# Choosing score banks for VectorE by a build-time account, queueing their later passes, and pairing row tiles in every filler step

## The chip, the cores and the metric

The kernel runs on one core of one Trainium2 chip. The metric is the time of one execution on the device, in microseconds, as the median of several runs; all seven inputs come from HBM and the output goes back there. A profile is one execution recorded by the hardware profiler. It has a span (first to last instruction) and a time of its own, which is a little longer than the span.

The engines are TensorE (PE in the profile, with its weight loads as PEld), VectorE (DVE), ScalarE (ACT), GpSimd (POOL) and SyncE (SP), which here only issues transfers. Each works through its own queue in order; they meet at semaphores that the framework sets from the tiles that instructions read and write.

## The reference

A transformer block on 2048 rows of 512 columns: layer norm, attention with 32 heads of 16, a residual, layer norm, a gated feed-forward part of 1792, a residual.

```python
qkv = (ln(x) @ wqkv)                       # 2048 x 1536 -> q, k, v, 32 heads of 16
p   = softmax(q k^T * 16 ** -0.5)          # 32 x 2048 x 2048
h   = x + (p v) @ wo
g, u = ln(h) @ w_gate, ln(h) @ w_up        # 2048 x 1792 each
out = h + (sigmoid(g) * u) @ w_down
```

The 32 x 2048 x 2048 exponentials, 134 million of them, are most of the elementwise work.

## The kernel before

**Steps.** Scores are made transposed, 128 keys by 512 queries at a time; such a piece fills one bank of PSUM. A unit is one head with one piece of keys (for the last two chunks of 256 queries, two pieces of keys, still one bank). Three units make a group, and the loop at the end of the program takes one group per step: 683 steps. `emit_scores` (from L746) writes one step: the score matmuls into one of two PSUM tiles `pss` of three banks, and one `activation` with Exp on ScalarE (L776) that turns the banks into bf16 probabilities in one of seven slots (`pt`, and pieces of `wd`, `stg` and `QTu` that lie idle at the time, so one line shows under several names). ScalarE works on one `pss` while TensorE fills the other.

**Cycles.** Four steps make a cycle. The twelve units of a cycle meet their values in three `emit_pv` calls (L839), which `plan_pv` puts six steps after the cycle's first: twelve matmuls, four at a time side by side in the array (tile position by columns), which add into the PSUM tile `acc`. A P.V matmul waits for the probabilities it reads. When a group of four heads is done, `emit_norm` (L816) copies `acc` out with VectorE (L820), and transfers bring the row sums through HBM and back.

**Filler.** Everything else that needs TensorE is a generator, `filler`, which yields a cost before each matmul: V tiles, K and Q projections, and for each chunk of queries the output projection, gate, up and down products. `emit_fill` draws from it at the end of each step, by a rate per step of the cycle (L737; 2, 2, 0 and 3 matmuls, none in the step of P.V) and by pauses ("gap", "at") that the generator asks for. All filler results go through one PSUM buffer, `pm`, which VectorE or ScalarE must empty before the next is started. The order of work on each queue is the order in which the program writes it; nothing reorders it later.

**Pairs.** A head has 16 columns, and a row of `QB` and `KT` for the bound, so the operands of two heads fit into the two halves of the 128 rows. Where `pairs` is set (L751), a score matmul takes 64 rows of the array at a tile position, and two of them from different halves run at once; otherwise it takes all 128 rows, with zeros for the other heads. Before, pairs are used in the first 44 steps, in every odd step, and in the third step of cycles that are in `twice`, except in the first two steps of a cycle with no filler (`idle`).

**Banks on VectorE.** ScalarE is relieved of some banks. In a step in `split` the activation takes two banks and VectorE makes the third's exponential by its own arithmetic, in five passes: the scores are scaled so that adding a constant and converting to an integer gives the bits of a power of two (`exp_bits`, L795), then the mantissa is cut out (L798) and a cubic is applied to it (L801, L804, L808). The first pass reads PSUM, so TensorE can't fill that `pss` again until it is done. `split` has the first step of each cycle, and `twice` adds the third step in every third or fourth cycle of some stretches. The later passes are put at fixed steps: one, two and three steps after the first, with `later`.

```python
split = set(range(8, G1, CYC))
...
later(i + 1, lambda: exp_first(*scratch))
later(i + 2, lambda: exp_second(*scratch))
later(i + 3, lambda: exp_third(pt[:, na, :], *scratch))
```

The intermediate results of the five passes lie in scratch space: one set for the first step of a cycle, and one in the `OT` tile not in use for the third.

## Time and profile before

| | |
|---|---|
| median of the runs | 966.58 us (966.09 to 969.06) |
| the profiled execution | 967.7 us, span 965.9 us |
| ScalarE busy | 897.1 us, 93% of the span |
| TensorE busy | 837.0 us, 87% |
| VectorE busy | 788.7 us, 82% |
| mean granted TensorE clock | 0.996 |
| banks on VectorE | 191 of 2048 |

A group's line in the profile gives the line of the kernel, the engine and operation, what it writes and reads with its shape and how often; then the busy time and the mean of one in ns; then the engine's idle time before these instructions, and what ended it. A busy engine can be one that waits inside a queue for nothing; what counts is which engine's idle time is short where the time is spent. TensorE's busy time counts each matmul with its whole latency, so matmuls that overlap in the array are merged, and a busy share of 90% is not the array at its peak. A window's line gives the same busy times for a stretch of time; the 40-step stretches of this kernel last 49 to 60 us.

A timeline's line gives the start, the time from the first's start to the last's end of a run of equal instructions, and in brackets how long the engine was idle before and what released it.

### The profile page before, as it was taken

To read this page: it belongs to the slowest core of one execution; us is meant where nothing else is said; L and a number is where in the kernel's file an instruction comes from. 1 tells how busy PE (TensorE), PEld (TensorE's weight loads), DVE (VectorE), ACT (ScalarE), POOL (GpSimd) and SP (SyncE) were. 2 spreads that over 40 slices of the span, in tenths; PEclk is the share of its full clock that TensorE was granted. 3 is DMA by queue.
4 is the path that set the end of the run, shared out by engine and by line. 5 is a ranking of instruction groups with operands and counts; after the bars stand their busy time and mean duration, and the time that the engine had idled before them with its cause. 6 is when DMAs were issued, how large, how long until landed. Compare 5 with 4: busy or idle time off the path is not lost.

```text
span 965.9 us, 17209 instructions
## 1 busy us (share of the span) xinstructions
PE 837.0 (87%) x6409; PEld 334.2 (35%) x6409; DVE 788.7 (82%) x1423; ACT 897.1 (93%) x770; POOL 39.0 (4%) x45
## 2 busy tenths in 40 slices
PE   4888888888889899988789999988788999998988
PEld 2221222222223232222222233222255555456646
DVE  8389999888888888898888888888898788777653
ACT  4799999999999999999999999989998999899862
POOL 4600000000000000000000000000000000000000
PEclk9999999999999999999999999999999999999999
DMA  5002341000003000001000000000010000110010
GB/s 161 20 1 56 114 95 38 15 15 3 15 26 103 15 15 16 16 12 27 15 26 27 16 16 16 12 17 26 16 29 24 16 12 13 27 32 16 9 35 12
DMA packets 37357, 28.39 MB, mean 29 GB/s; under 512 B 17692, under 2 KB 32632, under 8 KB 37272
## 3 DMA queue, kind: packets, MB, share of 16 engines
q1 hardware_dynamic: 35684, 25.71, 10.1%
q10 hardware_dynamic: 1588, 1.58, 0.5%
q8 instruction: 50, 0.82, 0.4%
q14 instruction: 35, 0.29, 0.1%
HBM read 20.31 MB, written 2.61 MB: 24 GB/s over the span
## 4 chain that ended last, share of the span: by engine, by line
PE 41%; DVE 26%; ACT 24%; issue 6%; DMA 2%; SPq 0%; ACTq 0%; DVEq 0%; POOL 0%
PE pss L765 20%; ACT pt L776 13%; PE acc L846 8%; PE pm L514 6%; ACT stg L776 4%; ACT wd L776 4%; DVE stg L795 3%; PE pm L530 3%; ACT QTu L776 2%; PE pm L490 2%; DVE st L137 2%; DVE reg L798 2%; DVE pt L808 2%; DVE y L801 2%; DVE y L804 2%
## 5 line engine op out<-in xcount | busy, mean ns | idle before, releaser
L765 PE MATMUL pss<-QB,KT 64*128 64x512 bf16 (+3 forms) x2560 | 473.2, 338 | 85.7 <-ACT pt L776 40.1
L776 ACT ACTIVATE pt<-pss 128x1536 bf16<-128x1536 f32 (+1 forms) x392 | 500.4, 1360 | 18.1 <-PE pss L765 14.8
L765 PEld LDWEIGHTS <-KT 64*128 64x128 bf16 (+1 forms) x2560 | 179.0, 95 | 345.4 <-issue 235.2
L776 ACT ACTIVATE stg<-pss 128x1536 bf16<-128x1536 f32 (+1 forms) x140 | 183.1, 1356 | 5.0 <-PE pss L765 4.2
L795 DVE TENSOR_SCALAR stg<-pss 128x512 int32<-128x512 f32 x123 | 84.8, 689 | 72.4 <-PE pss L765 60.5
L846 PE MATMUL acc<-pt,Vaug 128*17 128x512 bf16 (+1 forms) x1471 | 112.8, 339 | 5.8 <-DVE xs_all L820 3.7
L776 ACT ACTIVATE wd<-pss 128x1536 bf16<-128x1536 f32 (+1 forms) x80 | 103.8, 1392 | 1.4 <-PE pss L765 1.3
L776 ACT ACTIVATE QTu<-pss 128x1024 bf16<-128x1024 f32 (+1 forms) x71 | 95.5, 1345 | 1.7 <-PE pss L765 1.2
L801 DVE SCALAR_TENSOR_TENSOR y<-reg 128x512 f32<-128x512 f32 x123 | 85.2, 692 | 4.2
L804 DVE SCALAR_TENSOR_TENSOR y<-y,reg 128x512 f32<-128x512 f32 x123 | 84.2, 685 | 1.1
L846 PEld LDWEIGHTS <-Vaug 128*17 128x17 bf16 x2560 | 50.4, 89 | 97.4 <-issue 82.6
L530 PE MATMUL pm<-wd,reg 128*128 128x512 bf16 x224 | 62.4, 385 | 2.3 <-DVE ob L535 1.8
L514 PE MATMUL pm<-reg,reg 128*128 128x512 bf16 (+1 forms) x280 | 58.0, 337 | 6.4 <-DVE reg L527 6.2
L514 PE MATMUL pm<-reg,wu 128*128 128x512 bf16 (+1 forms) x280 | 58.1, 338 | 1.5 <-ACT sg L519 1.2
L798 DVE TENSOR_SCALAR reg<-stg 128x512 int32<-128x512 int32 x123 | 52.0, 423 | 2.0
L144 POOL TENSOR_TENSOR rs<-ve,pw_neg 128x1 f32<-128x1 f32 (+1 forms) x24 | 16.5, 687 | 894.5 <-DVE ve L142 893.9
L846 PE MATMUL acc<-stg,Vaug 128*17 128x256 bf16 (+1 forms) x564 | 50.7, 326 | 0.8 <-DVE stg L808 0.4
L527 DVE SCALAR_TENSOR_TENSOR reg<-sg,pm 128x512 bf16<-128x512 f32 x56 | 38.2, 683 | 14.5 <-PE pm L514 13.8
L808 DVE SCALAR_TENSOR_TENSOR pt<-y,stg 128x512 bf16<-128x512 f32 x70 | 47.8, 683 | 1.8
L519 ACT ACTIVATE sg<-pm 128x512 f32<-128x512 f32 x56 | 35.5, 633 | 10.3 <-PE pm L514 10.0
L795 DVE TENSOR_SCALAR wd<-pss 128x512 int32<-128x512 f32 x45 | 30.9, 687 | 13.0 <-PE pss L765 12.7
L163 PE MATMUL pm<-reg 128*128 128x512 bf16 x124 | 37.1, 387 | 1.2 <-DVE km L171 0.7
(115 smaller groups left out, 707.0 us busy)
## 6 DMA issues: line engine op xcount, KB each, us to landing
rb_all<-rd SPq DMA_DIRECT2D x96, 64.0 KB
reg<-in_A_x_dram SPq DMA_DIRECT2D x8, 256.0 KB
xr<-in_A_x_dram SPq DMA_DIRECT2D x16, 128.0 KB
out_dram<-ob SPq DMA_DIRECT2D x16, 128.0 KB
rb_all<-rd SPq DMA_DIRECT2D x60, 32.0 KB
KT<-stg SPq DMA_DIRECT2D x7, 256.0 KB
reg<-in_B_w_gate_dram SPq DMA_DIRECT2D x4, 448.0 KB
wu<-in_B_w_up_dram SPq DMA_DIRECT2D x4, 448.0 KB
```

The costliest lines, as they stand in the source:

```text
L163: nc.tensor.matmul(ps[:], lhsT=wqkv_sb[:, c, w0:w0 + P], rhs=xnT[:, c, n * QC:(n + 1) * QC], start=(c == 0), stop=(c == DC - 1))
L514: nc.tensor.matmul(ps[:, i * w:(i + 1) * w], lhsT=wt[:, c, f * P:(f + 1) * P], rhs=hnT[:, c, 0:w], start=(c == 0), stop=(c == DC - 1))
L527: nc.vector.scalar_tensor_tensor(out=out, in0=a, scalar=1.0, in1=b, op0=ALU.add, op1=ALU.mult)
L530: nc.tensor.matmul(ps[:], lhsT=hT[:, f, tt * P:(tt + 1) * P], rhs=wd[:, f, :], start=(f == 0), stop=(f == FC - 1))
L765: nc.tensor.matmul(pss[:, ui, h * w:(h + 1) * w], lhsT=KT[rows, g, kt * P:(kt + 1) * P], rhs=QB[n_qg % 2][rows, j, 0:w], start=True, stop= ...
L776: ex = nc.scalar.activation(out=pt[:, 0:na, :], in_=pss[:, 0:na, :], func=ACT.Exp, scale=DH ** -0.5 / QS)
L795: return nc.vector.tensor_scalar(out=e_bits, in0=src, scalar1=ONE_BITS, scalar2=0.0, op0=ALU.add, op1=ALU.max)
L798: nc.vector.tensor_scalar(out=e_man, in0=e_bits, scalar1=0x7FFFFF, scalar2=-0x40800000, op0=ALU.bitwise_and, op1=ALU.bitwise_or)
L801: nc.vector.scalar_tensor_tensor(out=e_pol, in0=m, scalar=PA, in1=m, op0=ALU.add, op1=ALU.mult)
L804: nc.vector.scalar_tensor_tensor(out=e_pol, in0=e_pol, scalar=PB, in1=e_man.bitcast(FP32), op0=ALU.add, op1=ALU.mult)
L808: nc.vector.scalar_tensor_tensor(out=dst, in0=e_pol, scalar=PC, in1=e_bits.bitcast(FP32), op0=ALU.add, op1=ALU.mult)
L846: nc.tensor.matmul(acc[32 * j:32 * j + VW, 0:w], lhsT=Vaug[:, kt, 4 * g + j, :], rhs=p[:, h * w:(h + 1) * w], start=(kt == 0), stop=(kt == ...
```

## The change

Four things change together.

1. A build-time account, `load`, adds up an estimate of the work written so far for VectorE (`book`: 118 plus the columns, per instruction) and for ScalarE (70 plus 0.805 per column). In each step `free_scratch` decides whether this step's third bank goes to VectorE: not before step 8, not in steps that end a group of heads (`norm_steps`), only if VectorE's account, with passes still queued, is at most 1300 ahead of ScalarE's (a third of that in the last step of a cycle), and only if a scratch set is free. `split` and `twice` are gone.
2. The passes after the first go into a queue, `lazy`. `emit_lazy` writes them, after the step's P.V matmuls and before its filler, when VectorE's account would stay within 500 of ScalarE's, and at the latest in the second step of the next cycle. The mantissa pass is an entry of its own.
3. There may be two or three scratch sets: the former ones, and for the last two chunks a part of `QTu`, whose layout is changed so that a chunk's columns lie together.
4. Pairs are used in every step that is not `idle`, whatever its place in the cycle. The filler's rate no longer differs in cycles of `twice` (the values there were the same as the first of the two rates).

```diff
+    FIX, ACT_FIX, ACT_COL = 118.0, 70.0, 0.805
+    ROOM, AHEAD = 1300.0, 500.0
...
-    QTu = const.tile([P, 4, S], BF16)
+    QTu = const.tile([P, NQC, 4, QC], BF16)
...
+    load = {"dve": 0.0, "act": 0.0}
+
+    def book(*cols):
+        for n in cols:
+            load["dve"] += FIX + n
...
             rates = (4.0 if i > 5 else 0.0, 4.0 if i < 6 else 2.0 if i > 16 else 0.0, 0.0, 4.0)
-        elif i - i % CYC + 2 in twice:
-            rates = (2.0, 2.0, 0.0, 3.0)
         else:
...
-        pairs = i < FIRST or (i % 2 == 1 or i - i % CYC + 2 in twice) and not idle
+        pairs = i < FIRST or not idle
...
-        na = n - 1 if i in split else n
+        scratch = free_scratch(i)
+        na = n - 1 if scratch else n
         ex = nc.scalar.activation(out=pt[:, 0:na, :], in_=pss[:, 0:na, :], func=ACT.Exp, scale=DH ** -0.5 / QS)
+        load["act"] += ACT_FIX + ACT_COL * na * QC
         if na < n:
-            scratch = scratch_of(i)
-            tc.declare_no_dep(exp_bits(pss[:, na, :], *scratch).ins, ex.ins,
+            name, e_bits, e_man, e_pol = scratch
+            tc.declare_no_dep(exp_bits(pss[:, na, :], e_bits).ins, ex.ins,
                               reason="both only read, from different banks")
-            later(i + 1, lambda: exp_first(*scratch))
-            later(i + 2, lambda: exp_second(*scratch))
-            later(i + 3, lambda: exp_third(pt[:, na, :], *scratch))
+            book(QC)
+            busy.add(name)
+            end = i - i % CYC + CYC + 1
+            lazy.append((end, QC // 2, lambda: exp_mantissa(e_man, e_bits)))
+            lazy.append((end, QC, lambda: exp_first(e_pol, e_man)))
+            lazy.append((end, QC, lambda: exp_second(e_pol, e_man)))
+            lazy.append((end, QC, lambda: (exp_third(pt[:, na, :], e_pol, e_bits), busy.discard(name))))
...
+    def scratch_sets(i):
+        c = next(c for c in reversed(range(NC)) if i >= first_step(c))
+        yield "e", early_scratch if i < GM else late_scratch
+        if c > 2:
+            yield "q", tuple(QTu[:, 1:3].rearrange("p a b q -> p (a b q)")[:, 2 * QC * k:2 * QC * (k + 1)]
+                             .bitcast(dt) for k, dt in enumerate((INT, INT, FP32)))
+        elif c == 0 or ("h", c - 1) in ready or i < first_step(c) + 28:
+            par = (c + 1) % 2 if c == 0 or ("h", c - 1) in ready else c % 2
+            flat = OT[par][:].rearrange("p g q -> p (g q)")
+            yield "o", tuple(flat[:, 2 * QC * k:2 * QC * (k + 1)].bitcast(dt) for k, dt in enumerate((INT, INT, FP32)))
+
+    busy = set()
+    lazy = deque()
+
+    def pending():
+        return load["dve"] - load["act"] + sum(FIX + cols for _, cols, _ in lazy)
+
+    def free_scratch(i):
+        load["dve"] = max(load["dve"], load["act"])
+        if i < 8 or i >= G1 or i in norm_steps:
+            return None
+        if pending() > (ROOM if i % CYC < 3 else ROOM / 3):
+            return None
+        for name, parts in scratch_sets(i):
+            if name not in busy:
+                return (name,) + parts
+        return None
+
+    def emit_lazy(i):
+        while lazy and (lazy[0][0] <= i or load["dve"] + FIX + lazy[0][1] <= load["act"] + AHEAD):
+            _, cols, fn = lazy.popleft()
+            fn()
+            book(cols)
...
-    split = set(range(8, G1, CYC))
-    twice = set()
-    for qc in range(1, NQC):
-        n0 = int(qc * SPC) + 52
-        for n in range(n0, min(int((qc + 1) * SPC) + 16, int(first_step(NC - 1)) + 14)):
-            if n % ((4 if n < n0 + 56 else 3) * CYC) == 0:
-                twice.add(n + 2)
-    split |= twice
...
+        norm_steps = {i for i, us in pv_due.items() for c, g, k, j in us if k == n_k(c) - 1}
...
             for fn in due.pop(i, []):
                 fn()
+            emit_lazy(i)
             if 1 <= i < NS:
                 emit_fill(i)
```

The remaining lines of the diff add a `book` call behind each piece of VectorE work (and one `load["act"]` behind the tanh), mark a chunk's output projection as done for the choice of scratch, and write `QTu` with its chunk index first.

## The prediction

> **What bounds the kernel now.** I read the page's busy shares first, then a table of windows cut at every 40th step, then the groups by shape, then the waits and the timeline. Shares over the whole span:
>
> ```profile
> PE 837.0 (87%) x6409; PEld 334.2 (35%) x6409; DVE 788.7 (82%) x1423; ACT 897.1 (93%) x770; POOL 39.0 (4%) x45
> ```
>
> Four windows of 40 steps (steps 40, 80, 320 and 640 on) and three of 3.4 us; the columns are length, then busy us and count of PE, weight loads, VectorE (DVE), ScalarE (ACT), POOL, then granted clock, DMA share and GB/s:
>
> ```profile
> 91.50:141.60 50.10, 43.46 (x274) 12.64 (x274) 45.65 (x83) 49.64 (x41) 0.00 (x0) 1.00 0.38 100
> 141.60:191.50 49.90, 42.03 (x268) 12.92 (x268) 44.17 (x79) 49.60 (x41) 0.00 (x0) 1.00 0.10 25
> 448.20:497.20 49.00, 38.12 (x250) 12.11 (x249) 42.89 (x73) 48.78 (x41) 0.00 (x0) 1.00 0.08 23
> 870.10:930.30 60.20, 54.78 (x631) 36.10 (x630) 42.38 (x79) 55.30 (x49) 0.59 (x1) 1.00 0.07 15
> ...
> 644.50:647.90 3.40, 2.04 (x13) 0.61 (x11) 3.33 (x7) 3.40 (x4) 0.00 (x0) 1.00 0.02 5
> 647.90:651.40 3.50, 3.43 (x14) 1.00 (x14) 1.30 (x3) 1.14 (x1) 0.00 (x0) 0.51 0.03 5
> ...
> 699.10:702.50 3.40, 2.06 (x20) 1.39 (x17) 3.16 (x6) 3.35 (x4) 0.00 (x0) 1.00 0.01 2
> ```
>
> In the first three ScalarE is busy 99% or more and VectorE 88 to 91%: the exponential sets the pace there. In the last ScalarE is at 92%: its scores come late. Prices, from the groups by shape:
>
> ```profile
> L776 ACT ACTIVATE pt<-pss 128x1536 bf16<-128x1536 f32 x281 | 400.3, 1479 | 12.0 <-PE pss L765 9.2 <-issue 1.2 <-DVE y L801 0.6
> L776 ACT ACTIVATE pt<-pss 128x1024 bf16<-128x1024 f32 x111 | 117.5, 1058 | 6.1 <-PE pss L765 5.6
> L801 DVE SCALAR_TENSOR_TENSOR y<-reg 128x512 f32<-128x512 f32 x123 | 85.2, 692 | 4.2
> L795 DVE TENSOR_SCALAR stg<-pss 128x512 int32<-128x512 f32 x123 | 84.8, 689 | 72.4 <-PE pss L765 60.5 <-ACT pt L776 5.1 <-ACT QTu L776 2.9
> L804 DVE SCALAR_TENSOR_TENSOR y<-y,reg 128x512 f32<-128x512 f32 x123 | 84.2, 685 | 1.1
> L798 DVE TENSOR_SCALAR reg<-stg 128x512 int32<-128x512 int32 x123 | 52.0, 423 | 2.0
> L808 DVE SCALAR_TENSOR_TENSOR pt<-y,stg 128x512 bf16<-128x512 f32 x70 | 47.8, 683 | 1.8
> ```
>
> So a bank on VectorE costs it 0.689 + 0.423 + 0.692 + 0.685 + 0.683 = 3.17 us of work and takes 1.479 - 1.058 = 0.42 us off ScalarE. The timeline has the two other things that matter here, the cost of a change of matmul shape and what a late VectorE does:
>
> ```profile
> 559.91 0.61 PE L765 MATMUL pss<-QB,KT 64*128 64x512 bf16 x3
> 560.45 1.04 PE L514 MATMUL pm<-reg,wu 128*128 128x512 bf16 x4
> 561.32 0.81 PE L765 MATMUL pss<-QB,KT 128*128 128x512 bf16 x3
> 562.06 0.39 PE L846 MATMUL acc<-stg,Vaug 128*17 128x512 bf16 x3
> ...
> 630.07 0.82 PE L765 MATMUL pss<-QB,KT 128*128 128x512 bf16 x3 [0.84 <-DVE stg L795]
> 631.99 0.38 PE L846 MATMUL acc<-pt,Vaug 128*17 128x512 bf16 x1 [0.56 <-DVE pt L808]
> 633.01 1.45 ACT L776 ACTIVATE pt<-pss 128x1536 bf16<-128x1536 f32 x1 [0.57 <-DVE y L801]
> ```
>
> **The change, part by part.** The built order of instructions gives the counts. SP and POOL issue the same instructions in the same order, so no transfer moves past another. TensorE keeps its order of work step by step (equal filler and P.V counts in every step). Banks on VectorE go from 191 to 213.
>
> *ScalarE.* 22 x 0.42 = 9.3 us less exponential, where ScalarE is the bound. By stretches of 40 steps the added banks are 1, 1, 2, 2, 2, 1, 0, 1, 2, 1, 0, 1, 1, 1, 1, 2, 3.
>
> *VectorE.* 22 x 3.17 = 69.8 us more; 788.7 becomes 858.5, 89% of the span. By stretch it is tight: steps 40 to 80 need 45.65 + 3.17 = 48.8 of 50.1 us (97%), 80 to 120 need 44.17 + 6.34 = 50.5 of 49.9 (101%), 320 to 360 need 42.89 + 6.34 = 49.2 of 49.0 (100%); 120 to 200 and 480 to 520 come to 95 or 96% (46.9 of 49.5, 47.7 of 50.2, 47.5 of 49.3), the others to 82 to 94%. No 40-step stretch of before runs VectorE above 91%, so what is lost beyond that is not shown. Bounds: it can be filled to 100% (80 to 120 grows by 0.6, 320 to 360 by 0.2), or never passes 91% (the six grow by 3.5, 5.6, 5.1, 2.0, 2.2 and 2.9 us). The nearest row is the one at 644.50, VectorE busy 3.33 of 3.40: I take 98%. Steps 80 to 120 then last 50.5 / 0.98 = 51.5, 1.6 more instead of 0.8 less; 320 to 360 last 50.2, 1.2 more instead of 0.8 less; 40 to 80 miss 0.1. Given back: 2.4 + 2.0 + 0.1 = 4.5 us.
>
> *The later passes.* Before, 168 banks are in the first step of a cycle of four and have their last pass three steps later; 23 are in the third step. P.V of a cycle stands six steps from its start. After, the banks spread 94, 51, 31 and 37 over the four steps, and passes may be put off to the fifth step. A bank of the fourth step has 3.17 us of passes, and 0.69 if another bank's first pass stands between, which the built order mostly shows. From the end of a late last pass to the exponential behind it takes 1.07 us above (the pass starts at 631.25 and takes 0.69; the exponential starts at 633.01). Together 4.9. ScalarE covers it with four exponentials: whole ones at up to 1.39 us (three begin at 399.18, the next at 403.34) and short ones at 0.97 (two begin at 403.34, the second ends at 405.76), 5.1 with one short, 4.7 with two. So the 37 banks hold ScalarE up by nothing, or by 4.9 + 0.69 - 4.7 = 0.9 us each where an evacuation stands between too: 0 to 33 us. The 23 third-step banks of before have as little room, and P.V's waits for L808 sum to 1.3 + 0.5 + 0.4 = 2.2 us, 0.10 each. P.V matmuls that carry a wait for VectorE rise from 48 to 120. I take 0.11 each, next to the only like case: 4 us. Behind the waiting matmul in TensorE's queue stands the next score triple, and the exponential waits for that.
>
> *Pairs.* Steps with pairs go from 433 to 660. A triple takes 0.81 us whole and 0.61 paired: 227 x 0.20 = 45 us of TensorE time less. Changes of shape cost: 561.32 to 562.06 holds two whole matmuls at 1.04 - 0.39 = 0.65, a third of it each, 0.43 in all, and one with a change, 0.31; so a change costs 0.09, and there are 1000 instead of 897: 103 x 0.09 = 9 us more. The Trainium skill, TensorEngine Tiling (Array Packing), Key Properties, says that a change of tiling mode drains TensorE, which speaks against this edit; the rows agree that it costs something, 0.09 us. Both are mostly idle time already. It counts where ScalarE waits for scores: 14.8 + 4.2 + 1.3 + 1.2 = 21.5 us in 49 waits. At best 49 x (0.20 - 0.09) = 5.4 us are gained, at worst 49 x 0.09 = 4.4 lost; I take 2.5 gained, since in most of these the triple itself is what is waited for.
>
> *First and last stretch.* From step 520 on ScalarE waits for TensorE's chain through the one pm buffer; of the 7 banks added there I count half as lost, 7 x 0.42 / 2 = 1.5 (between 0 and 2.9). In steps 8 to 24 the banks leave the steps whose V tile VectorE must evacuate; there the exponential behind starts late by 0.47 us (54.82 and 60.35 in the timeline), in four such cycles: 2 gained (between 0 and 2).
>
> *Nothing* is charged for QTu's new layout: it moves no instruction on any queue.
>
> *Sum.* -9.3 + 4.5 + 4 - 2.5 + 1.5 - 2 = -3.8 us on the profiled execution's 967.7 (span 965.9 and 1.8 around it), which is 1.1 above the runs' median of 966.58. On the median 962.8; I say 963.
>
> **The rivals.**
>
> *VectorE eats the gain (same).* If it holds only 96%, the stretches at 40, 80, 320 and 480 last 50.8, 52.6, 51.3 and 49.5, and with 0.2 at 120 that is 1.1 + 3.5 + 3.1 + 0.6 + 0.2 = 8.5 us given back, not 4.5: 967. Under 95% it passes over to slower (971 and more). For it: it idles 9% today wherever it is busiest. Against: the account puts off a bank when work is pending.
>
> *The last pass holds P.V (slower).* Place: the 37 fourth-step banks. Price: 0.57 us of ScalarE each, as at 633.01, where 0.11 is taken: 37 x 0.46 = 17, 980; at 0.4 each 974. It cancels the gain from 0.11 + 3.8 / 37 = 0.21 us each on. For it: the room counted above is nothing. Against it: 6 such waits in the trace.
>
> *The clock gate (slower).* A window with TensorE busy 2.04 of 3.40 us is followed by 3.5 us at a clock of 0.51, with ScalarE busy 1.14: 2.4 us lost. At 2.06 of 3.40 nothing followed. Pairs take TensorE time away: steps 80 to 120 fall to 42.03 - 20 x 0.20 = 38.0 of 49.9, 76%, near steps 320 to 360 now (38.12 of 49.00, 78%), which ran at full clock. Five such windows cost 12 us: 975; it decides from two on. The Trainium skill, TensorE: Matmul & The Clock Gate, Part 1, says that the clock falls to half after an idle window of some 3.4 us; the trace agrees on the half (0.51), not on the idleness: TensorE paused for 0.96 us at most before. By the page alone this rival has no place.
>
> *All of it is hidden (faster).* VectorE can be filled (0.8 given back), late passes cost nothing, and the half-clock window at 647.90 does not come again (2.4): -9.3 + 0.8 - 2.5 + 1.5 - 2 - 2.4 = -13.9: 952.7.
>
> That the edit does nothing is excluded by the built order.
>
> **How the numbers follow.** Forecast (960 to 964, all but its edge faster) 0.38; all hidden 0.12; VectorE at 96% 0.19, below 95% 0.05; P.V held 0.16; clock 0.10. 0.3% of 966.6 is 2.9 us, about what a measurement of this kernel can tell from no change. Faster 0.38 + 0.12 = 0.50; same 0.19; slower 0.05 + 0.16 + 0.10 = 0.31. The range leaves out the far end of the last pass's price and a little at the fast end: 953 to 975.
>
> **What would show it.** ScalarE's busy time falls by about 9 us. Steps 80 to 120 last over 50 us with VectorE at 98%, and steps 160 to 320 get shorter. P.V's waits for the last pass sum to 5 to 10 us; over 20 says that P.V is held. More than two half-clock stretches say the gate. The exponentials' waits for scores fall below 21.5 us if the pairs help. The prediction is wrong if VectorE stays well under 98% in steps 80 to 120 and 320 to 360 while ScalarE waits there, or if TensorE's pairs alone shorten stretches without added banks (240 to 280).

## The result, and the profile after

The changed kernel takes 1000.88 us (997.38 to 1005.29) against 966.38 for the kernel before in the same session: a ratio of 1.0348, 95% interval 1.0315 to 1.038. The forecast was 963 with a range of 953 to 975. The profiled execution of the changed kernel took 1000.15 us. The page of the changed kernel: the span, the busy shares, the granted clock in 40 slices, and the chain that ended last:

```profile
span 998.4 us, 17251 instructions
PE 820.7 (82%) x6313; PEld 282.1 (28%) x6409; DVE 853.6 (85%) x1533; ACT 891.9 (89%) x770; POOL 37.6 (4%) x45
PEclk9997999998898899999997999999989999999999
DVE 39%; PE 25%; ACT 19%; issue 10%; DMA 4%; SPq 1%; POOL 0%; DVEq 0%; ACTq 0%; POOLq 0%
```

Two things have changed character. The row of clock digits was all nines before; now there are 7s and 8s. And the chain, led by TensorE before (41%, VectorE 26%), now runs through VectorE for 39% of the span, although VectorE is busy 85% only.

Windows of 40 steps of the changed kernel, from steps 40, 80, 320 and 120 on (length, then busy us and counts of PE, weight loads, VectorE, ScalarE, POOL, then granted clock):

```profile
94.60:149.00 54.40, 43.26 (x268) 9.98 (x271) 48.71 (x88) 50.25 (x41) 0.00 (x0) 0.93 0.34 91
149.00:200.40 51.40, 38.49 (x264) 9.63 (x269) 48.34 (x87) 49.21 (x42) 0.00 (x0) 1.00 0.10 26
469.10:519.30 50.20, 36.72 (x246) 10.17 (x248) 47.81 (x81) 48.54 (x42) 0.00 (x0) 1.00 0.09 23
200.40:257.80 57.40, 44.37 (x264) 9.84 (x267) 48.80 (x84) 50.14 (x42) 0.00 (x0) 0.85 0.04 8
```

The second and third are the stretches that the prediction had computed as the tight ones: 51.4 and 50.2 us, 1.5 and 1.2 longer than before. The first and the last line are two of the others: at a mean clock of 0.93 and 0.85 they last some 4 and 8 us longer than before (50.1 and 49.5). By stretch, steps 0, 40, 120, 200, 360 and 520 give 3.1 + 4.2 + 7.9 + 5.8 + 6.0 + 3.6 = 30.6 of the 32.5 us, and each of them holds 5.9 to 17.1 us at half clock (before, the first held 3.4 and the others none). Half clock is not all of it: a run further below has nearly all of the half clock gone and more than half of this growth left. Short windows at the deepest of these places and at a second one:

```profile
242.40:245.80 3.40, 1.60 (x10) 0.30 (x8) 3.13 (x6) 3.40 (x4) 0.00 (x0) 1.00 0.00 0
245.80:249.20 3.40, 3.08 (x18) 0.54 (x16) 3.33 (x7) 3.15 (x3) 0.00 (x0) 0.50 0.00 1
249.20:252.60 3.40, 2.96 (x9) 0.46 (x10) 2.30 (x4) 1.34 (x2) 0.00 (x0) 0.50 0.03 4
...
324.20:327.70 3.50, 2.01 (x13) 0.45 (x9) 2.56 (x6) 3.50 (x4) 0.54 (x1) 1.00 0.00 0
327.70:331.10 3.40, 2.63 (x18) 0.53 (x18) 3.28 (x6) 2.73 (x2) 0.00 (x0) 0.50 0.00 0
331.10:334.50 3.40, 3.18 (x11) 0.78 (x10) 2.60 (x5) 1.02 (x1) 0.00 (x0) 0.50 0.02 5
```

In both places a window in which TensorE has few matmuls (x10, x13) while ScalarE is fully busy is followed by 3.4 us or a multiple of it at a clock of 0.50, and within that time ScalarE runs out of scores (1.34 and 1.02 us busy of 3.40). The loop has 14 such half-clock stretches, some 75 us in all; before it had two of 3.4 us.

The exponentials by shape, which set the size of the saving:

```profile
L798 ACT ACTIVATE pt<-pss 128x1536 bf16<-128x1536 f32 x276 | 395.3, 1480 | 30.5 <-PE pss L786 22.6 <-issue 2.7 <-ACT pt L798 2.3
L798 ACT ACTIVATE pt<-pss 128x1024 bf16<-128x1024 f32 x116 | 123.5, 1064 | 3.5 <-PE pss L786 3.2
```

The prices have not moved (1480 and 1064 ns, before 1479 and 1058). What has moved is the idle time in front of the whole ones, 30.5 us where it was 12.0. The same in the waits of the changed kernel, first TensorE's P.V matmuls (L905) for VectorE's last pass (L864) and for its emptying of `acc` (L876), then the exponentials for scores (us, times, longest):

```profile
PE acc L905 <- DVE pt L864: 7.7, 11, 1.5
PE acc L905 <- DVE xs_all L876: 7.7, 17, 1.0
...
PE acc L905 <- DVE wd L864: 2.0, 4, 0.8
...
PE acc L905 <- DVE stg L864: 1.1, 2, 0.9
...
PE acc L905 <- DVE QTu L864: 0.2, 1, 0.2
```

```profile
ACT pt L798 <- PE pss L786: 25.9, 43, 2.6
ACT stg L798 <- PE pss L786: 10.6, 17, 1.5
...
ACT wd L798 <- PE pss L786: 7.3, 12, 1.3
ACT QTu L798 <- PE pss L786: 6.2, 8, 1.8
```

P.V waits for the last pass 7.7 + 2.0 + 1.1 + 0.2 = 11.0 us in 18 waits (before 2.2 in 6), for `acc` 7.7 us (before 4.1). The exponentials wait for scores 50.0 us in 80 waits, against 21.5 in 49. One such wait in the changed kernel's timeline, the counterpart of the one shown at 631.99 before:

```profile
176.14 0.67 DVE L884 TENSOR_TENSOR OT<-xs_all,rb_all 128x512 bf16<-128x512 f32 x1
176.55 0.60 PE L905 MATMUL acc<-wd,Vaug 128*17 128x512 bf16 x6
176.74 0.67 DVE L860 SCALAR_TENSOR_TENSOR OT<-OT 128x512 f32<-128x512 f32 x1
...
177.45 0.69 DVE L864 SCALAR_TENSOR_TENSOR pt<-OT 128x512 bf16<-128x512 f32 x1
178.19 0.39 PE L905 MATMUL acc<-pt,Vaug 128*17 128x512 bf16 x4 [1.04 <-DVE pt L864]
178.52 0.61 PE L786 MATMUL pss<-QB,KT 64*128 64x512 bf16 x3
179.22 2.52 ACT L798 ACTIVATE wd<-pss 128x1024 bf16<-128x1024 f32 x2 [0.76 <-PE pss L786]
```

The output scaling at 176.14 stands in front of the last two passes, P.V waits 1.04 us, the score triple stands behind P.V, and the exponential loses 0.76 us.

One sum is used below. Back to back, exponentials start 1.333 us apart (whole) or 0.905 us apart (short), and a tanh adds 0.478. Added up over the steps this is the least that ScalarE needs in the loop: 491 whole, 191 short and 49 tanh make 850.8 us before, 469, 213 and 49 make 841.4 after. The rest of the loop's time, its **loss**, was 45.6 us and is 87.0. So 22 exponentials that are 0.43 us shorter save 9.4 us, and 41.4 us went.

### The profile page after: what moved, and what is told of

Its sections match the earlier page's. It is cut to its first block, busy times and chain, and to the rows that moved or that the text cites. A ratio compares the mean times of both kernels' runs of the same rounds, so it can differ in the third digit from the quotient of the medians.

```text
span 998.4 us, 17251 instructions
## 1 busy us (share of the span) xinstructions
PE 820.7 (82%) x6313; PEld 282.1 (28%) x6409; DVE 853.6 (85%) x1533; ACT 891.9 (89%) x770; POOL 37.6 (4%) x45
## 4 chain that ended last, share of the span: by engine, by line
DVE 39%; PE 25%; ACT 19%; issue 10%; DMA 4%; SPq 1%; POOL 0%; DVEq 0%; ACTq 0%; POOLq 0%
PE pss L786 11%; ACT pt L798 10%; PE acc L905 5%; ACT stg L798 4%; DVE stg L849 4%; DVE y L857 4%; PE pm L532 3%; DVE pt L864 3%; DVE reg L852 3%; DVE y L860 3%; ACT QTu L798 2%; PE pm L550 2%; ACT wd L798 2%; DVE wd L860 2%; DVE wd L849 2%
## 5 line engine op out<-in xcount | busy, mean ns | idle before, releaser
L786 PE MATMUL pss<-QB,KT 64*128 64x512 bf16 (+3 forms) x2555 | 425.8, 347 | 109.1 <-ACT pt L798 52.0
L786 PEld LDWEIGHTS <-KT 64*128 64x128 bf16 (+1 forms) x2560 | 126.3, 95 | 400.0 <-issue 314.4
L905 PE MATMUL acc<-pt,Vaug 128*17 128x512 bf16 (+1 forms) x1471 | 123.9, 355 | 13.8 <-DVE pt L864 7.7
L849 DVE TENSOR_SCALAR stg<-pss 128x512 int32<-128x512 f32 x114 | 78.5, 689 | 36.2 <-PE pss L786 18.0
L798 ACT ACTIVATE QTu<-pss 128x1536 bf16<-128x1536 f32 (+1 forms) x71 | 95.4, 1343 | 7.1 <-PE pss L786 6.2
L905 PEld LDWEIGHTS <-Vaug 128*17 128x17 bf16 x2560 | 51.6, 91 | 110.3 <-issue 96.8
L860 DVE SCALAR_TENSOR_TENSOR y<-y,reg 128x512 f32<-128x512 f32 x114 | 78.6, 690 | 3.2
L857 DVE SCALAR_TENSOR_TENSOR y<-reg 128x512 f32<-128x512 f32 x114 | 78.7, 690 | 2.9
L550 PE MATMUL pm<-wd,reg 128*128 128x512 bf16 x200 | 57.3, 382 | 7.3 <-DVE ob L555 4.0
L905 PE MATMUL acc<-stg,Vaug 128*17 128x256 bf16 (+1 forms) x564 | 53.7, 338 | 2.6 <-DVE xs_all L876 1.5
L852 DVE TENSOR_SCALAR reg<-stg 128x512 int32<-128x512 int32 x114 | 48.2, 423 | 2.5
L864 DVE SCALAR_TENSOR_TENSOR pt<-y,stg 128x512 bf16<-128x512 f32 x66 | 45.2, 684 | 0.9
L905 PE MATMUL acc<-QTu,Vaug 128*17 128x512 bf16 (+1 forms) x285 | 39.1, 342 | 1.2 <-DVE xs_all L876 0.8
```

What stands on the lines that cost most here:

```text
L550: nc.tensor.matmul(ps[:], lhsT=hT[:, f, tt * P:(tt + 1) * P], rhs=wd[:, f, :], start=(f == 0), stop=(f == FC - 1))
L786: nc.tensor.matmul(pss[:, ui, h * w:(h + 1) * w], lhsT=KT[rows, g, kt * P:(kt + 1) * P], rhs=QB[n_qg % 2][rows, j, 0:w], start=True, stop= ...
L798: ex = nc.scalar.activation(out=pt[:, 0:na, :], in_=pss[:, 0:na, :], func=ACT.Exp, scale=DH ** -0.5 / QS)
L849: return nc.vector.tensor_scalar(out=e_bits, in0=src, scalar1=ONE_BITS, scalar2=0.0, op0=ALU.add, op1=ALU.max)
L852: nc.vector.tensor_scalar(out=e_man, in0=e_bits, scalar1=0x7FFFFF, scalar2=-0x40800000, op0=ALU.bitwise_and, op1=ALU.bitwise_or)
L857: nc.vector.scalar_tensor_tensor(out=e_pol, in0=m, scalar=PA, in1=m, op0=ALU.add, op1=ALU.mult)
```

## The experiments

Two theories stood at the start. **Clock**: the pairs shorten TensorE's stretches of work, the granted clock falls, and this is the loss. **VectorE**: the loss comes from the account and the queue, by the number of banks, the late last pass, or the order in which the passes stand in VectorE's queue. Each time is followed by its ratio to the kernel before in the same session, with the 95% interval.

### Pairs against the account

The changed kernel with the old rule for pairs:

```diff
-        pairs = i < FIRST or not idle
+        pairs = i < FIRST or (i % 2 == 1 or i - i % CYC + 2 in twice) and not idle
```

> The changed kernel with the old rule for pairs; the account, the queue and the 213 banks stay. If the pairs take TensorE's activity below what holds its clock (theory A), the half-clock stretches fall from 14 to at most 4 and the time to 962 to 970 us. If late VectorE passes hold TensorE and the pairs are innocent (theory B), the low windows stay: 8 or more half-clock stretches and 985 us or more. If both are needed (theory C), 970 to 985.

988.18 us, 1.0219 (1.0196 to 1.0242). The mean clock is back at 0.994, and yet most of the loss stays. The six stretches named above still grow by 2.2 + 3.5 + 4.6 + 2.0 + 2.8 + 1.5 = 16.6 of their 30.6 us, where they now hold 2.8, 0, 3.4, 0, 0 and 0 us of half clock. The reverse, the kernel before with the new rule for pairs alone:

> The kernel before with only the new rule for pairs: 191 banks at their old places, old passes. Theory A: 8 or more half-clock stretches, 980 to 1000 us. Theory B: no more than 3 half-clock stretches, 960 to 968 us, since pairs only save TensorE time. Theory C: 3 to 6 half-clock stretches and 966 to 978.

977.54 us, 1.0108 (1.0078 to 1.0138), mean clock 0.970, 62 us of half clock in the whole execution. The stretches without half clock are 0.1 to 0.5 us shorter than before (the last 1.1), those with it 0.4 to 4.5 longer. Windows of this run:

```profile
193.50:247.60 54.10, 44.29 (x268) 10.36 (x267) 40.73 (x70) 50.31 (x42) 0.00 (x0) 0.87 0.04 9
232.70:236.10 3.40, 1.95 (x13) 0.48 (x12) 2.18 (x4) 3.40 (x4) 0.00 (x0) 1.00 0.00 0
236.10:239.50 3.40, 3.00 (x18) 0.58 (x15) 1.98 (x3) 3.23 (x3) 0.00 (x0) 0.50 0.01 2
```

VectorE is busy 40.73 of 54.10 us here, and its instructions and their order are those of before, so it is not the cause: a thin window (x13), then half clock, and steps 120 to 160 last 54.1 us instead of 49.5. So both theories hold, the clock for about 10 to 13 us (the second figure is 1000.88 - 988.18) and VectorE for 21. To see whether more work on TensorE would buy the clock back, the changed kernel issued its third bank's score matmul twice in the even steps (the second writes the same values into the same bank):

```diff
+        if pairs and i >= FIRST and i % 2 == 0:
+            parts += [p for p in parts if p[0] == order[2][0]] if n > 2 else []
```

> The changed kernel, all pairs kept, with the third bank's score matmul made twice into the same bank in every even step after the first 44 (same values; TensorE gets some 300 x 0.22 = 65 us more work). Theory A: the extra work holds the clock, so more work is faster: at most 5 half-clock stretches and 965 to 980 us. Theory B: the extra matmuls change nothing or cost: 998 us or more.

1006.96 us, 1.0406 (1.0377 to 1.0435). Half clock in the whole execution fell from 79 to 45 us, and the time rose: read so, the doubled matmuls cost more on the path than the clock gave back. Useful work does better: pairs kept out of the steps with thin filler, in the kernel before:

```diff
-        pairs = i < FIRST or (i % 2 == 1 or i - i % CYC + 2 in twice) and not idle
+        pairs = i < FIRST or (i % 2 == 1 or i - i % CYC + 2 in twice or state["rate"]) and not idle
```

> The kernel before, with pairs in every step in which the filler is in a feed-forward part (dense filler), and the old rule elsewhere: 569 steps with pairs instead of 433. If pairs cost only by the clock (theory A), no half-clock stretch is added here and the stretches shorten as in the run of the pairs alone, by some 0.4 us in six of them: 963 to 966 us. If pairs cost by their changes of shape, 967 to 970.

965.71 us, 0.998 (0.9963 to 0.9997), with 20 us of half clock in the whole execution (before 9). It has 569 steps with pairs; before there were 393 by the rule at L751, not the 433 of the prediction and of the expectation. This settles what the pairs alone cost: the built program has 991 changes of matmul shape, the run with pairs everywhere 1000 and the kernel before 897, so nearly all of the changes are here and the 10 us are not. Stretches without half clock are up to 0.9 us shorter. (One, steps 440 to 480, is 1.7 us shorter, but there the half-clock stretch of before at 648.0 did not come.) This is the one version that beats both kernels, by 0.2%, which is just clear of noise.

### How much of the account is in the number and place of the banks

From here on all runs but one, which is named, have the old pairs, and the mean clock of the profiled execution stays at 0.988 or more except where a figure is given. Fewer banks, by a higher cost of an instruction in the account:

```diff
-    FIX, ACT_FIX, ACT_COL = 118.0, 70.0, 0.805
+    FIX, ACT_FIX, ACT_COL = 160.0, 70.0, 0.805
```

> As the first kernel here (old pairs, account, queue), but the account takes 160 instead of 118 per VectorE instruction, so 206 banks instead of 213. If VectorE at 100% costs what the account gains (steps 80 to 120 and 320 to 360), this is 1 to 3 us faster than the first kernel; if not, up to 3 us slower, for 7 banks of 0.42 us back on ScalarE.

980.54 us, 1.0135 (1.0091 to 1.0179). The built program has 197 banks (89, 50, 32 and 26 over the four steps), not the 206 that the expectation names. With 16 banks fewer than the account takes otherwise it is faster by 7.6 us, but with only 6 banks more than the kernel before it is still 13 us slower. Next, no bank in the fourth step of a cycle:

```diff
-        if i < 8 or i >= G1 or i in norm_steps:
+        if i < 8 or i >= G1 or i in norm_steps or i % CYC == 3:
```

> Old pairs, account and queue, but no bank in the fourth step of a cycle: 190 banks (135, 27, 28 and 0 over the four steps), about as many as before. If the fourth-step banks, whose last pass comes too late for P.V, make most of the 21 us of the account (theory P), 965 to 972 us, and P.V's waits for the last pass fall from 10 to under 4 us. If it is the delay of the passes by the queue, wherever the bank is (theory Q), 978 us or more.

979.81 us, 1.0133 (1.0107 to 1.0159). The waits of P.V for the last pass fall to 1.2 us, below those of before (2.2), and 8.4 us come back. So the late last pass is not the other 13. Whether it is the 8 is open: this run also has 23 banks fewer, and the run before it gave back nearly as much with 16 fewer, 26 of its banks still in the fourth step and 3.1 us of such waits. The opposite, passes never put off:

```diff
-    ROOM, AHEAD = 1300.0, 500.0
+    ROOM, AHEAD = 1300.0, 1e9
```

> Old pairs and the account's places (217 banks, 39 in the fourth step), but every pass is written in the step of its bank, behind the first pass. Theory P: the fourth-step banks have no less work ahead of P.V but nothing between their passes, so a part comes back, 976 to 985 us. Theory Q: nearly all comes back, 962 to 970. If VectorE being full is what costs (theory F), no better than 986.

1155.52 us, 1.1947 (1.1926 to 1.1969), clock 0.945. All passes of a bank then stand in the step of the bank itself. TensorE's waits in this run:

```profile
PE acc L905 <- DVE xs_all L876: 46.5, 24, 4.1
PE pm L532 <- DVE reg L546: 43.1, 36, 2.4
```

It is VectorE's other duties, emptying `acc` and the one filler buffer `pm`, that are late, not the passes: P.V waits for the last pass 1.3 us. That shifted the question to VectorE's order.

### The queue, at the old places

The banks at the very places of before, with the new queue:

```diff
-        if pending() > (ROOM if i % CYC < 3 else ROOM / 3):
+        if i not in split:
```

> Old pairs, banks at the places of before (190 of the 191), passes by the new queue. Theory P: 965 to 970 us, as before, since the last pass still has room. Theory Q: the queue alone costs, 975 us or more.

981.63 us, 1.0153 (1.0131 to 1.0176): 15 us lost with 190 banks. Bringing the deadline of the passes back to the third step (`end = i + 3`):

> As the run with the old places and the queue (981.6 us), with one thing changed: the passes are due three steps after their bank, instead of in the second step of the next cycle. P.V then has the last pass at least one step earlier for third-step banks, and two for first-step banks. If P.V held by passes put off to the deadline makes the 15 us, 966 to 971 us and P.V's waits for the last pass under 4 us, from 11.4; if it is the bursts of passes written in one step, 976 us or more.

988.06 us, 1.021 (1.018 to 1.0239), 6 us more instead of 15 less. The edit does less than the expectation says: a third-step bank's passes were due three steps later already, so only first-step banks change. P.V's waits for the last pass fall only from 11.4 to 4.7 + 2.7 + 2.4 = 9.8 us, and TensorE's waits for the next bank's first pass rise from 5.7 to 12.5. So an earlier deadline does not help; that late passes are innocent does not follow from this run. The reverse: the account chooses the banks (210 of them, with `ROOM` 1800), and each pass stands in its old step, none earlier.

```diff
+            lazy.append((i + 1, QC // 2, lambda: exp_mantissa(e_man, e_bits)))
+            lazy.append((i + 1, QC, lambda: exp_first(e_pol, e_man)))
+            lazy.append((i + 2, QC, lambda: exp_second(e_pol, e_man)))
+            lazy.append((min(i + 3, end), QC, lambda: (exp_third(pt[:, na, :], e_pol, e_bits), busy.discard(name))))
```

> Old pairs; the account chooses the banks (210; over the four steps 116, 42, 51 and 1; the limit raised to 1800 to keep the count), but the passes stand at the old fixed steps: two one step later, one two steps later, the last three steps later. If the putting off of passes is what costs (theory Q), 958 to 968 us: 19 banks of 0.42 us gained and VectorE's loss at 100% against it. If VectorE being full is what costs (theory F), 975 us or more.

988.19 us, 1.0213 (1.0184 to 1.0241): the account's places and its 19 further banks cost as well, with the passes in their old steps. The one run with other pairs, with FIX 160, no bank in the fourth step and the pairs of the best run, has 198 banks:

> A bid for better than both: old pass steps, the account with 160 per VectorE instruction, no bank in the fourth step (198 banks: 108, 44, 46 and 0), and pairs in the feed-forward parts only. If Q and the clock are the two causes, 958 to 965 us; if VectorE full costs by itself, 968 or more.

979.07 us, 1.0122 (1.0095 to 1.015). No setting of the account that was run reaches the kernel before.

### VectorE's order alone

The last runs keep the 190 or 191 banks at the old places, and TensorE's instructions in exactly the order of before; they differ only in where the passes stand on VectorE. First with every pass in its old step:

> The changed kernel with the old rule for pairs, the banks at the old places and each pass written in its old step (the first two passes one step after the bank, the next two steps after, the last three steps after; nothing earlier). Only the new layout of the query tile, the new choice of scratch and the account's bookkeeping are left of the change; TensorE's order is that of before and 46 of VectorE's 1425 instructions stand elsewhere. Theory A (the time from which the queue writes the passes is the whole loss of the two runs at the old places, 981.63 and 988.06): 965 to 969 us. Rival B (the new layout or the shared scratch costs by itself): 975 or more.

972.90 us, 1.0052 (1.003 to 1.0074), 6 us more than expected. Leaving aside which scratch is written, the order on VectorE differs from that of before in 14 places only (the expectation of the next run says 15). Each time the last instruction of a layer norm (`xn`) now stands in front of a pass where it stood behind it. VectorE's timeline before, and then in this run:

```profile
304.54 0.15 DVE L142 TENSOR_SCALAR ve<-mv 128x1 f32<-128x1 f32 x1
304.61 0.68 DVE L804 SCALAR_TENSOR_TENSOR y<-y,reg 128x512 f32<-128x512 f32 x1
305.33 0.69 DVE L808 SCALAR_TENSOR_TENSOR stg<-y,stg 128x512 bf16<-128x512 f32 x1
305.94 0.54 DVE L148 TENSOR_SCALAR xn<-reg,mv,rs 128x512 bf16<-128x512 f32 x1
```

```profile
304.90 0.15 DVE L146 TENSOR_SCALAR ve<-mv 128x1 f32<-128x1 f32 x1
304.97 0.68 DVE L858 SCALAR_TENSOR_TENSOR y<-y,reg 128x512 f32<-128x512 f32 x1
306.09 0.55 DVE L152 TENSOR_SCALAR xn<-reg,mv,rs 128x512 bf16<-128x512 f32 x1 [0.43 <-POOL rs L148]
306.55 0.68 DVE L862 SCALAR_TENSOR_TENSOR stg<-y,stg 128x512 bf16<-128x512 f32 x1
```

The layer norm waits for GpSimd's power; the pass used to fill that wait, and now it stands behind it and starts 1.65 us after `ve` (304.90 to 306.55) where it was 0.79 (304.54 to 305.33). At 308.0 the clock falls to half for 3.4 us, and the stretch of steps 200 to 240 is 2.6 us longer. Two more half-clock stretches, in steps 320 to 360 and 360 to 400, go with 1.6 and 3.3 us; steps 440 to 480, which held the one of before at 648.0, are 1.6 us shorter. VectorE's waits for GpSimd are 2.3 us here, 0.3 before, and 5.6 in the changed kernel. The test is to write the passes ahead of what is due in a step:

```diff
-            for fn in due.pop(i, []):
-                fn()
             emit_lazy(i)
+            for fn in due.pop(i, []):
+                fn()
```

> The run with the old places and the old steps (972.90 us) again, with the step's passes written ahead of what is due in the step instead of behind it. In that run VectorE's order differed from the one of before in 15 places only, each time a pass that stood ahead of a layer norm's last instruction and then stood behind it, where VectorE waits for GpSimd (2.3 us in 6 waits, before 0.3 in one). Theory N (these 15 swaps, with the half-clock stretches behind them, are the 6 us): 965 to 969 us, and VectorE's waits for GpSimd back to about 0.3 us. Rival: the passes now also stand ahead of the row sums' reciprocals, and if the swaps are not the cause the time stays at 971 to 975 us.

969.03 us, 1.0016 (0.9998 to 1.0034), and VectorE waits for GpSimd 0.3 us again. That is the upper edge of what was expected: with the 14 swaps undone most of the 6 us is back, although in 46 other places VectorE's order is now not that of before, most of them a pass and a row sum's reciprocal. So the swaps with the layer norm are most of the 6 us, and the new layout and scratch cost nothing that can be told from zero. Now the account's drawing forward, never later than before:

> The same, but a pass may be written before its old step when the account says that VectorE is less than 500 columns ahead of ScalarE; none is later. Theory A1 (passes drawn forward, next to the score bank and to each other, stand ahead of VectorE's emptying of projection and output banks): 977 to 990 us, waits of TensorE for VectorE's reading of its accumulators above those of before. Theory A2 (only lateness costs, by holding P.V): 964 to 969 us, and the waits of P.V for the last pass stay near the 2.2 us of before.

984.19 us, 1.0166 (1.0136 to 1.0196). P.V's waits for the last pass are 1.6 us, below those of before, so nothing is late. TensorE's waits for VectorE's emptying of `acc`, before and in this run:

```profile
PE acc L846 <- DVE xs_all L820: 4.1, 9, 1.0
```

```profile
PE acc L903 <- DVE xs_all L874: 10.9, 17, 2.0
```

Twice as many of the copies of `acc` are late, up to 2.0 us. In front of all 17 VectorE works without a pause, and at least one pass is among that work; before, this was so in 4 of 9. Here is one of them, first as it stood before (L804 is the fourth of the five passes, L820 the copy), then in this run (L858 and L874):

```profile
561.26 0.69 DVE L801 SCALAR_TENSOR_TENSOR y<-reg 128x512 f32<-128x512 f32 x1
561.87 0.68 DVE L527 SCALAR_TENSOR_TENSOR reg<-sg,pm 128x512 bf16<-128x512 f32 x1
562.51 0.69 DVE L820 COPY xs_all<-acc 128x512 f32<-128x512 f32 x1
563.12 0.68 DVE L804 SCALAR_TENSOR_TENSOR y<-y,reg 128x512 f32<-128x512 f32 x1
```

```profile
571.50 0.69 DVE L858 SCALAR_TENSOR_TENSOR y<-y,reg 128x512 f32<-128x512 f32 x1
572.11 0.68 DVE L546 SCALAR_TENSOR_TENSOR reg<-sg,pm 128x512 bf16<-128x512 f32 x1
572.70 0.68 DVE L874 COPY xs_all<-acc 128x512 f32<-128x512 f32 x1
...
573.44 0.39 PE L903 MATMUL acc<-QTu,Vaug 128*17 128x512 bf16 x2 [0.61 <-DVE xs_all L874]
```

The fourth pass, which had time, now stands in front of the emptying of the filler's bank and of `acc`, and the next P.V matmul waits 0.61 us. And in one block, all four passes in the third step, never earlier:

> The same places, but all four passes of a bank written together three steps after it, none earlier: the last pass's step is that of before, the other three are drawn back to it, so that one block of some 2.2 us stands in VectorE's order. Theory A1' (a block of passes is what costs, wherever it stands): 975 to 990 us, and the waits for the last pass rise above 5 us since it now stands behind three others. Theory A1 (only what is drawn forward costs): 965 to 971 us.

1035.76 us, 1.0692 (1.066 to 1.0725), clock 0.970, the dearest order for the same work and far above both ranges. Its timeline has the block and who pays:

```profile
295.35 0.42 DVE L850 TENSOR_SCALAR reg<-stg 128x512 int32<-128x512 int32 x1
...
297.25 0.69 DVE L862 SCALAR_TENSOR_TENSOR pt<-y,stg 128x512 bf16<-128x512 f32 x1
298.08 0.69 DVE L847 TENSOR_SCALAR stg<-pss 128x512 int32<-128x512 f32 x1
...
298.83 1.27 PE L786 MATMUL pss<-QB,KT 128*128 128x512 bf16 x3 [2.07 <-DVE stg L847]
...
300.20 1.45 ACT L798 ACTIVATE pt<-pss 128x1536 bf16<-128x1536 f32 x1 [2.17 <-PE pss L786]
```

From 295.35 to 297.94 VectorE is in the block; the first pass of the next bank, before which TensorE can't fill that score tile again, waits for its turn until 298.08, TensorE loses 2.07 us and ScalarE 2.17. Over the whole run TensorE waits 35.8 us for first passes (before 7.7), and P.V waits 16.5 + 6.7 + 5.2 = 28.4 us for the last one, which now stands behind three others; 13 half-clock stretches in the loop come with it. Last, whether the place of the queue's passes ahead of the step's filler matters, and whether the layer norm's order explains the queue:

> The run with the queue at the old places (981.63 us), with the queue's passes written behind the step's filler instead of ahead of it, so that VectorE's work on a bank that the filler has finished stands ahead of the passes of that step. If the passes' standing ahead of the filler's evacuations is the loss: 968 to 974 us, and fewer waits of TensorE for VectorE's reads. If the loss is in the late last pass and in the spread over the cycle: 979 to 986 us.

995.67 us, 1.0283 (1.0254 to 1.0312), clock 0.979: worse, with P.V's waits for the last pass at 11.3 + 7.4 + 4.2 = 22.9 us.

> The same edit in the run with the queue at the old places (981.63 us, VectorE waits for GpSimd 5.5 us in 9 waits). Theory N: 970 to 976 us, as the swaps' 6 us come back and what the account draws forward stays. If drawing passes forward is what costs and the layer norm does not matter: 979 to 984 us.

979.89 us, 1.0123 (1.01 to 1.0146), where the queue behind had 1.0153 (1.0131 to 1.0176): the two can hardly be told apart. VectorE still waits 3.5 us for GpSimd, so layer norms still stand where they wait. Of the queue's 15 us at the old places the layer norm's order is a small part at most here; the run with passes only drawn forward lost as much without any late pass.

## Why the prediction was wrong

It was wrong in sign, by 38 us, and two steps failed.

*ScalarE, -9.3: held.* The least that ScalarE needs fell by 9.4 us, and so did the durations of the exponentials added up (929.9 to 920.5). Its busy time fell only from 897.1 to 891.9: exponentials that follow each other directly overlap, busy time counts the overlap once, and with more waits between them the overlaps shrank from 75.9 to 70.2 us. So 9 us less busy time was not the sign to look for.

*VectorE, +4.5: two sizes came out, by luck.* Steps 80 to 120 and 320 to 360 grew by 1.5 and 1.2 us where 1.6 and 1.2 were forecast. But VectorE was busy 48.34 of 51.4 and 47.81 of 50.2 there, 94 and 95%, not 98. The text said that it would be wrong if VectorE stayed well under 98% while ScalarE waits: that happened, so a VectorE filled to the brim is not what made these stretches longer. Nor did steps 160 to 320 get shorter as a whole: 200 to 240 grew by 5.8 us.

*The later passes, +4: the first failed step.* The waits of P.V for the last pass came to 11.0 us, just above the 5 to 10 that were named, and taking the fourth-step banks away, with 23 banks fewer, gave back 8.4. This term was too small, by half at the most. What has no term at all is the order of the other passes. The step took a pass to be load, with one deadline at P.V; it did not ask what stands behind each pass in VectorE's queue. With the same banks, the same work and TensorE's order untouched, the order alone moved the time from 969 (passes in their old steps, ahead of the layer norm) to 981.6 (the queue), 984.2 (drawn forward only) and 1035.8 (in one block). The forecast followed what is queued behind the waiting P.V matmul, and not what is queued behind the moved passes: copies of `acc`, the layer norm, the next bank's first pass.

*Pairs, -2.5: the second failed step.* Alone they cost 10 us, and 12.7 on top of the account. The prices of a triple and of a change of shape were not the issue: with pairs alone, stretches without half clock got shorter, most by 0.1 to 0.5 us. (Steps 240 to 280, named as a sign of being wrong if they did, were 0.4 shorter with pairs alone and 1.2 in the changed kernel.) The exponentials' waits for scores, which were to fall below 21.5 us, rose to 50.0. The step that failed is the argument against the rival of the clock gate: steps 80 to 120 at 76% busy were held against steps 320 to 360, which run at 78% and full clock. The share over 40 steps says nothing here. The clock is decided over 3.4 us; steps 80 to 120, at 75%, did keep full clock, and those on both sides of them, at 80 and 77%, did not. The rival was there with its mechanism, and a chance of 0.10 was too low. It came by number and not by price: with pairs alone, the eight stretches that hold half clock hold 17 windows of 3.4 us and are 15.7 us longer, about 0.9 a window where 2.4 was named. "By the page alone this rival has no place" went by one passage only; the last section has another of the same part of the Trainium skill.

*First stretch, -2, and late stretch, +1.5.* The first grew by 3.1 us, and by 2.2 with the old pairs, so the gain is seen in neither. From step 520 on 3.6 + 0.0 + 2.3 + 1.0 = 6.9 us were lost, in the stretches with half clock; with the old pairs it was 2.9.

*Nothing for QTu's layout: held*, as the run with old places, old steps and passes ahead of the layer norm shows (1.0016, 0.9998 to 1.0034).

*All hidden* assumed that the half-clock window would not come again. It came 14 times.

The two losses nearly add up: the account with its queue 21 us, the pairs 10 to 13, and both together 34.5 (1000.88 - 966.38). How the 21 split between number, places and order of the banks stays open in part: the queue at the old places costs 15, and the account's places with passes in the old steps cost 21, of which 6 come at the old places too, by the layer norm's order; and these overlap. That the pairs bring the half clock is shown in both directions, by adding them to the kernel before and by taking them out of the changed one. That the half clock follows from thin windows is read from where it falls; no run set the windows' content on purpose without also changing the path, since the doubled matmuls did both.

## What to carry to other kernels

On an engine that does a pipeline's chores in order, a piece of work with time to spare must not stand in front of one that has none: list what stands behind each moved instruction and who waits for it, before counting how full the engine is. A balance of loads kept at build time knows nothing of this. Here the spread of one bank's passes over the steps was worth 66 us against one block, and choosing the banks by the account gained nothing. Work taken off TensorE is not free where it is already thin: judge the clock by the thinnest 3.4 us, not by the mean share.

## What the runs showed of the hardware that was not expected

The clock looks at windows of fixed length. The half-clock stretches of all these runs that are over before the trace ends last 3.413, 6.827 or 10.240 us, whole multiples of one window, and in each run they start on one grid, to within 2 ns. The Trainium skill, TensorE: Matmul & The Clock Gate, Part 1, says that the window is free-running and 3413 ns long; the trace agrees to the nanosecond. Its table of states has the clock fall after an idle window, and a later passage of the same part tells of a kernel whose TensorE was idle only briefly, often, between groups of matmuls, and whose clock swung all the same. The runs here are of the second kind: none of the windows in front of half clock was idle throughout.

Each matmul can be counted by the time that its columns take to stream (0.22 us for 512 at full clock, from three-matmul rows), with matmuls that run side by side counted once. In all traces together 109 half-clock stretches begin between 80 and 930 us. The windows in front of them have shares of 0.05 to 0.50; 93 lie under 0.45. The share is not a sharp bound: 55 windows under 0.45 kept the clock, some matmul records are missing from a trace, and the counts shift with the 0.22 (at 0.2157 us, more windows of both kinds fall under 0.45). Two paired matmuls count once, so by this count pairing lowers the share while the same work gets done.

The price of such a window can be read without any change to the program. In the 52 executions of the kernel before that were measured next to the experiments, the granted clock lay between 0.988 and 1.000 and the time between 973.57 and 965.65 us, and the two go together (correlation -0.95): by a straight line through them, each 3.4 us of half clock costs about 1.0 us.

And the kernel before sat close to that edge: with 14 swaps of two neighbouring instructions on VectorE, the profiled execution has three half-clock stretches in the middle of the loop where there had been one. The number differs from one execution to the next; the median clock was 0.994 with the swaps and 0.998 without, which by that price is some 2 of the 6 us.
